# Another table of priorities for the planned instruction order of an attention and two feed-forward layers

## The chip, the cores and the metric

The kernel runs on one core of a Trainium2 chip. The metric is the device time of one execution in microseconds (us). TensorE, VectorE, ScalarE, GpSimd and SyncE appear in the views as PE, DVE, ACT, POOL and SP; PEld is the loading of weights into PE, and SPq is SP's queue of transfers.

## The reference

Attention in float32 over 2 batches of 8 heads, 768 positions and 64 dimensions, where a query sees only the keys of its own hash bucket, then a gated layer of width 1536 behind a normalisation, then a layer of width 2048:

```python
q_bits = (np.einsum('bhsd,dk->bhsk', q, proj) > 0)          # 6 bits make the bucket
mask = q_bucket[:, :, :, None] == k_bucket[:, :, None, :]
scores = np.where(mask, scale * np.matmul(q, k.transpose(0, 1, 3, 2)), -1e9)
attn = softmax(scores);  x = np.matmul(attn, v)             # (1536, 512) tokens
xn = x / rms(x) * rms_g
x = (silu(xn @ w_gate) * (xn @ w_val)) @ w_out              # 512 -> 1536 -> 512
return (np.maximum(x @ w_in, 0) ** 2) @ w_out2              # 512 -> 2048 -> 512
```

## The kernel before, in words

**Attention** goes in 96 slots: 16 heads with 6 tiles of 128 queries each. A slot is a short chain over the engines. PE makes the scores of the tile (`S`, L627: four matmuls of 384 columns, two parts of the operands by two halves of the keys). DVE takes their maximum and copies them out of PSUM (L638, `Pa` or `Px`). ACT makes the bias (L647) and the exponentials (L656). Then the probabilities are split into two 16-bit parts and transposed, by one of two ways. In the "a" slots, 66 of them, ACT makes the high part (`hla`, L376), POOL the low part by a subtraction (L385, `hla<-Pa,hla`), and a DMA on SP's queue transposes both (`Ta`, L668). In the 30 "x" slots PE transposes (L675), ACT and DVE read the result out of PSUM. Last, PE multiplies with the values (`O`, L701, 18 matmuls).

**Each head** needs its own preparation ahead of its first slot: loads of keys (`rk`, L466, 384 KB) and queries (`rq`, L469, 192 KB), the split of keys and queries into a high part (L378, L376 or L380) and a low part (L385, `k<-rk,k` and `q<-rq,q`), a hash by PE (L508), its bits by DVE (L517, `q<-S,cst`), and a small DMA that brings the bits to the keys (L525). Values are loaded for two heads at a time (`vr`, L552, 384 KB), scaled (L603) and split (L380 or L376 and, for the low part, L385, `vl<-vr,ones`).

**The normalisation** of a half batch (L940 to L975) makes the sums of squares on ACT (L940), scales them on DVE (L945), raises them to -1/2 on POOL (L950) and corrects the result by one Newton step in four small DVE instructions (L957, L959, L961 and L965, which writes `rr`). Three tiles of `xall` are then multiplied by `rr`, on DVE (L973), ACT (L971) or POOL (L975); PE transposes them (L983), and ACT and DVE split them into `xTA` (L991, L389). Only behind the normalisation of the first half can the first layer's products start (L1122 into the hidden units, L1234 and L1245 out of them). Weights come as 64-bit numbers (`wraw`, L1053, 512 KB a block) and are made into two parts by ACT, DVE and POOL (L1066 to L1086, L376, L385).

**The order** of all this isn't written by hand. `plan_all` gives each operation a rank, the engines that may run it, and a cost. `Plan.shift` adds a number from the table `SHIFTS` to each rank, and `Plan.run` is a list scheduler: it emits, one after the other, the ready operation that can start first by the costs, and on a tie the one with the lowest rank. Which engine runs an operation, and each engine's order, come out of that. The order is fixed at build time; on the chip each engine takes its instructions in that order and waits on semaphores.

```python
moved = int.from_bytes(raw[2 * n:2 * n + 2], "little", signed=True)
o.rank = (round(o.rank * 32) + moved) / 32 + n * 1e-6
...
if best is None or (t, o.rank) < best[0]:
    best = (t, o.rank), n, eng, c
```

37 matmuls on a tile of zeros (`idle`, L455) stand between the first slots.

Of the kernel before, what the change touches and what calls it, by code (L numbers as in the profile page):

```python
# [109 lines left out]


SHIFTS = (
    'c-rk(XLMCX*WOdktw0h==t##<rAw6>qy-QHO7ERF2nYfax)dW-q?Z5+2!tXv2neCPAQ&M60VEL+L%26LLUQjtWoGtw)_'
    'VWF-@otQw-(P{XU#fu*37JR_I{pu_GD}<8i<iZqt!xZj7OnShLdK5GDC}uQ&>IpFcisu58VkZG)mfYdqRg*sZc<V4HKA'
    'abRj>HGIEo+EYn3CuCe;bcg14shH*fgG<J*G#w1ZzZzz|Oxnh7doeY;xMVz%qJQ4q5SIkqgmhhW(MKttQOf)pnYAKb~1'
    'wB@jxFURJW$S>s6Mhu$V}|p*AbK?`8Dq_J#&(gee}%j7o`@3PT2*Bqu~oQKHV%^~tVnS{4zuEEH!;iViGARNl480w2nU'
    ')^<Uw37_rM|R5A%C7nr<hvNto<ZSM;Wi=gN;mog?+hP|M+WwDm3_rD=IcrRxB&r_8`OSc12p8<q_QF$;#MZ{<e$9jym*'
    'U@;tH_oV}tVh}r$I@VKcPq!GqVsG9OCP0FbVH9EqjKJAuU6`Ynqtn%oxB$1Q!RkxAu6LJ9RC6^SZ>e8lzFLNr;I<Kje5'
    'iw;+I!8!nwC=y!G73I?N&dS=`dfOg#f(|6QQD7Nfwd2a)j1N)m9$qHjdC5SOqO~>MP(&C`ryKO{L;NbyKVmUQ&Q9;2q3'
    '_Y;{&HwNL$v^i{gK!i*uY&ed|SbE4`l;>BEeqzXwM-h?*T7qeAsM-;gwd+RAG0%9Q3h;`KCC$+np1J2VtdRF$8sn&<Gq'  # L120
    'Rba5qMex^J{?8{B*hg&PS9PP8k=b<e8lsNOqQi3sg2mj>MnD{5;8_sHeZv`a<F-oe}Pl*s!>K7)_S@{b}?@_pQ#jel(n'
    '_?S#f5R+$o#VmN?32z|P?lW1Uu=wbmz?k+2Z|3NMq>%yc>d%8NKdl1TPM-vZ@fXt*;>6MggvXj(aVM6co{;!`kjt@z9w'
    'F0adcGg(MA*P1Sp^<Tt9^`1EjTEdS~=?jD*zcXH#k04PmqRN<0&9!2u`94-=?~oz-cj^XKGppP6*i>$_N}$WUq$-mBdN'
    'le)7qf^sXB-#H#b0nM`~~9@%u;3psAav8hjF_Zg$v*hbyU4j2lPhzr=p2-CryCv_#rkomZ@}kLF^J!g%^ryi|k5kt36b'
    'abc2kxEU`<UCN4UjkcKP?ljJ_JR6hq*jD{)$DjUn>Ju(uT<0E~MK2{%(BUvVCB2Sv@^lD}rT+>gZ4zKi6m_-J_5j8^Jt'
    '=H6AkqBxSmB=vC*_eXYttMJCtr}xST~YvVjBP|3%U~?NubKQJ-y~jA8B75WAWzYc;0Z&(67L~f9SZc;-Z0!SdK+_$RH('
    '=r8fCoY$a8(Jaa$jv=fW%(vUFVOec_!>B1i`Po6Uwcq-5|o^d-$yf;S!F*iinx{(y}jMRk*}!kU=nu^Fmer&ake_??V2'
    'i`o06^D%sM;ZaqbGzsnz705*pMLOVq-k5Dtr;Tw$!!d;qaE07z%`~packr%}CU-z8b}sA>|CXJtXXXS0p(pg`d&xJXm;'
    'OGUk{zu|g$s=RbhW-2yU<8zXspJjqLR_vDrQ8Hu~=5^#i8nZJKLr)nRG(U9EL#7$Yz*m9G3UhT=Nd3s=x6ATx?vlPN+J'
    '@a`rWTC7Wr#VX@F3tgjKL*5Ly^4KDJ=&Qj1y41|B!V7roQ*gU?@+_2G1BwO)omBoBgiYaO_p2RtrD^poj`9i!jpNkZ%h'  # L130
    '@*rPdw@s%K{G{x<rej^FC7T$WtbV(WKo3O79-GN+x2FuDYh}&v1B|Zj$5}?S#p%_wmQny;+cw3<;6Rqv5K)-+EbMi4Xi'
    '@;C)IGL^_6I4^P>&+#8k6}jOQ0=zW7;Olcz{u%OxArkE{&Ql(qAm7yCqgbzFk*T1V6e)_rl1wj-0|G<Hp16t~16kst@-'
    'D)A{%a8UGR<v|lA1;gPaO$9|w)=EXm9lW*2DMzYtY&}NWafNh)ljJj8<(`3Ku`y`KL-$l=H?Vv)nbzU2$zyc!7`#eb%R'
    '9Du_J&yPCB#B)_eC5^YT;{jBwU3qqTdIL@>g_6@E>xMeiE$2@8Ck>lyNv&wX`x}KLGoQ_7jt>{%WF1Rwq>tzL`EYdUz6'
    'KX)z04Vm9qXQ(Z~!Xw^?Og~}Mu6!l^?j8qNOJeWoo28Zx#&RA7NWs^?u2~EQY8Yv&Chs3GwSyN;e_OV@6ztR%KfKzlfo'
    '2Dw_Ok9Ce=mgS|g=t@vE90RB3=A)kW7uw5pH-6sNN?Dnl4J|zVOiv!ED2?0KP-@y>0K<uaWam6ta9)JSPstcD^*<`l^4'
    'hz(UIIyQ$!3Ipl->4Y$}JtbJVRH<e@w%_sPwoGXs2RmWE4msN5qbVs++JznJ-WPz<v(6oo&L-{4&=!2N2e+(1TPEy%_='
    'Eyg{Fe`qkZT1}Vxz>SljK2frb3aD@GnR_alb*E)9&oNKlkzcZB+6(5V*ObAFl7FBT|K9nK{z5gC<Ge&Nn2(P!j?$TQKH'
    '0=O8^!gRW*O&ZdKI>?O{}TW1(Ntn{f@X2-m8C3zaZyGA|GZB(KAGpF`r$gSIGufjJet9Z%oxH&{%q!EaK&iG~<?5TMLp'
    'VtT-*^4r^QW^G2Lrfp=hANRW?l%rUkZXZZ=1O+TkWGQsr)spGk>Ro3FQNUa^qq({keepPGhK&_S*rWM#h@`U{DsNksX+'  # L140
    'QED9POLPYMGre3I{Rx!ctxIz*I^|&<4BTCwIPlvtSAeSZz3DYsgAp5M4%Nd%lztj#0RoA4#f^?r<rU7^5*ejydr*#zgk'
    'MH*PiB8XYaCFWI)tW`9v(#qIkBwY83q;@|wJ?UDi@qbyk!wp*{0UJErnnk&K)r@Oku@iiJ9yLIqxqRb?319SHb8q%B;v'
    'n1|QpBe5l$&o8qbdC%xES~@?`S&o%rFG#&WN47FAj}37u`Z4?&covxCJB8~5S$R#_;=ChhD;(c|7Xqt&?for$Pt{r~ZO'
    '#=05`2sOqy2+?Q)x4PHvfG7^}M32M#0`UJqtPnCl?zKTJ1XT%GI+9y^-1aPVa8lP)}@;*7&98v3sJ+>8|J9;TrELQ6OD'
    'ig9ltu1w}nGJw-g9dHUg*H<Pq=TJwVP?lInmnBhufMG8*1UU-)|_dB-->xa7)Obq|4u&h;8FRC2DCfW;iIXotuQ!q>2k'
    'aOg7(V2D#ZpR4Chf%=<ZIk)|33BoYZqh60_ec$OMue<GkSxZMWEP2yWjh*_SLIfjiAAuNdO=QN7W!#C-r%b-l|3Qf&?('
    'y2auVw!yUB<0k)5|CHaBnLyY#u-L1(BNfFc$XFc<e?TT&hC<8}Pb5pUnoy^OC|H#tPDhaBmX4X`{MRjtT0FjOkE(8{_i'
    'Vj*p8XZ-?ABgIK9Ug3YLL{^F(BlWcFo}H>3&QhcB6$Y$cHjfkJ8kq$b)DV%VvM?X(i92FBPg0StxstGV#3;uex8JEtH}'
    '<fdSJ<)CDxz(}-$Ze>)j5ohq^5{r<B3Oga@NNtBFkoUST4~nh~?TTd;lvQlbk<k?HmPSF#imTc;dn3yo*&yAC8*R20LE'
    'T@s8t=>rQcQ)C3spwrcKt2FH#0{5GV!lW?FX7o1+xuBkX!>b(RB-VOMeyyAcH!`$s?Z)|dIg=<=jcR3U@hSU4*#qQT`l'  # L150
    'UH^942`{WoErNT);Olpy5tt!BHG*TYpmvVmvMRAiL9oU%%Vx0b88g9czv#`rLz?;#}Db3$R3!b^>Z^akBp}`v~hF+RJY'
    'yaLK;hYX>G}e<TxyYkaiQ&5XnZZHuO>NmB_&gCC<WY>rhl{{H=H$Oo%!R5LMj00MBDAo`g9#2BNh;aWCw_=c=UkJFX=)'
    ';TP2fo{E@=dl4^W`-lT<k@}mQR<&VH;Ai+<_EMad2pEA9`3ca7Wfgl;tdTgGx6$@vgr3jK3|zp?=A)vqVo9;q5o_3ZF%'
    'qiqNQcw0&KK=SAbF1YWNYAaQX_vObXBz+=Ny}SeqUd*&p&}24YXDd^3%!GKolJvI7j|^bv`dhudyf`@#YonotNXhOCP8'
    ')d8M%2n}K+kto8Nved%B7@BON*{|${IJ&D5MuX22c{8Rn9zl9nP+g0{IAGv0bG&(hW4Q8_%>@04iNw`-=<VnA<!{>{~8'
    'MLSEvs&RIYpQRkty6{I3pUF4t1uS6I_-PvGklXp-G92$GNd)@O}FF5;CkC5tXG{e(UA#-v<)4Nnq!2q91F-vXh%DRV(9'
    '05Cw)z-ku@}hym5?Ulzzugk*?$%-Y@J3(d1)N19mx2SqbE#yMW!sDcWab23g6blS$eFI*W6@h<9OcNEg>OR>k=_&oJ(g'
    '4!Bu!k|Q?1^C41eOUJMij;G+@|0d7KLOPDT%eT|wcr@pNtd3`~6?Q4?jAx)D|Bb)LyK9MXh(E@9aD`unOVEm@l5AV6M`'
    '<l>H&lYHWHVWU{t<O+En&2(N(Zs_j(8%V61O0i<&baj9L?2#BwfQjZ5{1Fy*!C7#$(ut?;>ez5UmDVY`-Rn5o%8D2JlU'
    'Ldu=AMAd^<5|E6=owcr+=Lb6Fe=%$iGv2X^qk{<SrRE58%>(HC@Qs?P;93FbC((oSMR!MeOH3XKkXvhve#7<BZMq|lP5'  # L160
    'EJn|Iu`t7nwo>Jh%NzAXaw|NYv30#7U#h}^9#5k(x5F#w~8|^T<|-+j6a7`FeP*bx7&TiD!B`PvU<>)R&mtn04x;kaTP'
    '@341A!Lsw;&%^kS&VeKsf7S!=D+>M34;^+q(_H>*M;E2u7!DEpKx!KY+4Rx3Pi9KnHD*H~!1FmBoYtq5e;9q4~zE?iUp'
# [1318 lines left out]
```

## Time and profile before

| | us |
|---|---|
| median of 3 runs | 787.13 (787.03 to 789.05) |
| the profiled execution | 786.7 |
| its span, first to last instruction | 784.9 |
| PE busy | 761.1 (97%) |
| PEld busy | 690.0 (88%) |
| DVE busy | 686.5 (87%) |
| ACT busy | 452.6 (58%) |
| POOL busy | 230.6 (29%) |

The time of an execution is its span and 1.8 us around it. Busy time of PE counts each matmul from its issue to its end, and neighbours overlap, so 97% isn't PE at its peak. The granted clock is the share of TensorE's full 2.4 GHz that the chip allowed in a stretch; 0.50 is its lower level, 1.2 GHz. "Idle before" in an instruction's row is the time in which its engine stood still ahead of it, with the one that ended it.

### The profile page before, as it was taken

The page shows a single profiled execution, that of the slowest core. Times are in us where ns is not written, and L with a number is a line of the kernel's source. Part 1 is how long each engine was busy: PE and PEld are TensorE (multiplying, and loading weights), DVE is VectorE, ACT ScalarE, POOL GpSimd, SP SyncE. Part 2 cuts the span into 40 slices and gives each one's busy share as a digit, 9 for nine tenths or more (in the row PEclk, how much of TensorE's full clock was granted, in tenths as well). Part 3 has the DMA queues.
Part 4 walks back from the last instruction along what each step waited for, and adds up shares of the span by engine and source line. Part 5 has one row for each costly group of instructions (what it writes and reads, how often), then busy time and mean ns, then how long its engine had stood idle before and what let it go on. Part 6 is the DMA issues. An engine that isn't in the chain of part 4 may idle for free.

```text
span 784.9 us, 14412 instructions
## 1 busy us (share of the span) xinstructions
PE 761.1 (97%) x5401; PEld 690.0 (88%) x5401; DVE 686.5 (87%) x1341; ACT 452.6 (58%) x897; POOL 230.6 (29%) x196
## 2 busy tenths in 40 slices
...
GB/s 251 130 172 169 207 153 141 143 190 195 230 205 163 198 164 197 97 129 164 108 146 96 134 139 134 130 82 130 58 54 53 54 108 53 54 55 53 28 1 161
DMA packets 127726, 100.65 MB, mean 128 GB/s; under 512 B 106548, under 2 KB 108596, under 8 KB 127656
## 3 DMA queue, kind: packets, MB, share of 16 engines
...
## 4 chain that ended last, share of the span: by engine, by line
PE 76%; DVE 11%; ACT 5%; DMA 4%; issue 2%; POOL 1%; SPq 0%; ACTq 0%; DVEq 0%; POOLq 0%
PE mo L1122 37%; PE mo L1245 17%; PE mo L1234 12%; PE S L627 4%; PE O L701 3%; DMA Ta<-hla 3%; DVE Pa L638 2%; DMA wraw<-in_w 1%; PE S L508 1%; DVE Px L638 1%; DVE Tx L385 1%; ACT Px L656 1%; ACT Pa L656 1%; ACT hla L376 1%; PE mo L455 1%
## 5 line engine op out<-in xcount | busy, mean ns | idle before, releaser
L1122 PE MATMUL mo<-xTA,wih 128*128 128x384 f32 (+1 forms) x512 | 138.4, 351 | 0.0
L1122 PE MATMUL mo<-xTD,wih 128*128 128x384 f32 (+1 forms) x512 | 136.8, 348 | 0.0
L385 POOL TENSOR_TENSOR hla<-Pa,hla 128x768 f16<-128x768 f32 x66 | 112.3, 1704 | 68.3 <-ACT hla L376 58.8
L1261 DVE TENSOR_TENSOR acc<-acc,mo 128x512 f32<-128x512 f32 (+1 forms) x164 | 100.9, 617 | 22.2 <-PE mo L1245 17.5
L1122 PEld LDWEIGHTS mo<-xTD,wih 128*128 128x128 f32 x512 | 93.3, 188 | 5.0
L1122 PEld LDWEIGHTS mo<-xTA,wih 128*128 128x128 f32 x512 | 92.8, 188 | 5.0
L1158 ACT ACTIVATE mt<-mo 128x512 f32<-128x512 f32 x48 | 28.7, 598 | 117.6 <-PE mo L1122 117.5
L627 PE MATMUL S<-k,q 76*128 76x384 f32 (+1 forms) x384 | 87.0, 354 | 6.3 <-DVE Px L638 2.8
L380 POOL TENSOR_SCALAR wih<-wv 128x512 fp32r<-128x512 f32 x16 | 9.9, 622 | 278.1 <-DVE wv L1086 265.3
L1122 PE MATMUL mo<-xTA,wil 128*128 128x384 f32 (+1 forms) x256 | 89.4, 349 | 0.0
L1122 PE MATMUL mo<-xTD,wil 128*128 128x384 f32 (+1 forms) x256 | 89.0, 348 | 0.0
L627 PEld LDWEIGHTS S<-k,q 76*128 76x128 f32 (+1 forms) x384 | 65.2, 190 | 10.9 <-DVE Pa L638 4.8
L1066 ACT ACTIVATE wv<-wraw 128x512 f32<-128x512 f32 x82 | 54.6, 671 | 21.0 <-DMA wraw<-in_w 19.2
L638 DVE TENSOR_SCALAR_CACHE_REDUCE Pa<-S 128x768 f32<-128x768 f32 x66 | 62.7, 950 | 3.5 <-PE S L627 2.6
L656 ACT ACTIVATE Pa<-Pa,b 128x768 f32<-128x768 f32 x66 | 62.3, 944 | 5.6 <-DVE ss L945 1.5
L1162 DVE TENSOR_TENSOR mu<-mt 128x512 f32<-128x512 f32 x48 | 33.3, 693 | 36.9 <-ACT mt L1158 36.9
L1234 PE MATMUL mo<-yl,woh 128*128 128x384 f32 x192 | 64.4, 335 | 1.2 <-DVE yl L385 1.2
L1234 PE MATMUL mo<-yh,woh 128*128 128x384 f32 x192 | 65.0, 339 | 0.3 <-DVE wol L385 0.3
L1234 PE MATMUL mo<-yh,wol 128*128 128x384 f32 x192 | 64.3, 335 | 0.0
L1082 DVE SCALAR_TENSOR_TENSOR wv<-wraw,wv 128x512 uint32<-128x512 uint32 x82 | 57.7, 708 | 1.0
L1086 DVE SCALAR_TENSOR_TENSOR wv<-wraw,wv 128x512 uint32<-128x512 uint32 x82 | 55.9, 686 | 0.4
L376 ACT CAST hla<-Pa 128x768 f16<-128x768 f32 x66 | 54.8, 834 | 2.2 <-DMA Ta<-hla 1.6
...
## 6 DMA issues: line engine op xcount, KB each, us to landing
wraw<-in_w SPq DMA_DIRECT2D x104, 512.0 KB
rk<-in_k SPq DMA_DIRECT2D x14, 384.0 KB
vr<-in_v SPq DMA_DIRECT2D x8, 384.0 KB
...
q<-q SPq DMA_DIRECT2D x15, 192.0 KB
rq<-in_q SPq DMA_DIRECT2D x14, 192.0 KB
Ta<-hla SPq DMA_TRANSPOSE x66
rk<-in_k ACTq DMA_DIRECT2D x2, 384.0 KB
```

The lines of the kernel that those rows point to most:

```text
L376: nc.scalar.copy(out_, in_)
L385: engine[eng].tensor_tensor(out=out_, in0=in0, in1=in1, op=ALU.subtract)
L627: nc.tensor.matmul(sp[:, hf, 0:TB], d[a][0:kr, t * 128:(t + 1) * 128], d[b2][0:kr, hf * TB:(hf + 1) * TB], start=(n == 0), stop=(n == 1),)
L638: nc.vector.tensor_scalar(out=e["P"].rearrange("p (a b) -> p a b", a=2), in0=e["sp"][:, :, 0:TB], scalar1=-1e9 / SCALE, scalar2=None, op0= ...
L656: nc.scalar.activation(e["P"], e["P"], AF.Exp, bias=e["b"], scale=SCALE)
L1066: nc.scalar.activation(t, f32(wst[m]["hi"]), AF.Abs)
L1082: nc.vector.scalar_tensor_tensor(out=t, in0=hi, scalar=0xC0000000, in1=t, op0=ALU.bitwise_and, op1=ALU.bitwise_or)
L1086: nc.vector.scalar_tensor_tensor(out=t, in0=lo, scalar=29, in1=t, op0=ALU.logical_shift_right, op1=ALU.bitwise_or)
L1122: nc.tensor.matmul(ps, a[:, c * 128:(c + 1) * 128], b2[:, c, :], start=(c == 0 and n == 0), stop=(c == 3 and n == 2),)
L1234: nc.tensor.matmul(po, a[:, dc * 128:(dc + 1) * 128], b2, start=(j == 0 and n == 0), stop=(j == len(fs) - 1 and n == 2),)
L1245: nc.tensor.matmul(po, a[:, tt * 128:(tt + 1) * 128], b2, start=(j == 0 and n == 0), stop=(j == len(fs) - 1 and n == 2),)
L1261: nc.vector.tensor_tensor(out=ac, in0=ac, in1=st["p"], op=ALU.add)
```

## The change

The table `SHIFTS` is another; nothing else is changed. Its rows are packed numbers and say nothing to a reader:

```diff
 SHIFTS = (
-    'c-rk(XLMCX*WOdktw0h==t##<rAw6>qy-QHO7ERF2nYfax)dW-q?Z5+2!tXv2neCPAQ&M60VEL+L%26LLUQjtWoGtw)_'
...
+    'c-rk(XLMFYx88eBdEb|WmIwrpA`um731A>dM>>cCQuKoa5RsyRPw666Kro;nQl+RADFGo!wNW(`gFr;86d{0+kn+CgoS'
...
 )
```

All operations are the same, and there are as many on PE (7160) as before. Nearly each engine's order is another. A few operations change engine: DVE has 1246 instructions (1247 before), ACT 897 (892), POOL 201 (201). The changed file is one line shorter above the code, so its line numbers are one lower: L384 there is L385 before.

**First place: DVE and POOL at the normalisation of the first half.** DVE before, from the scaled sums of squares (L945) to the multiplication of a tile (L973):

```order
L945 TENSOR_SCALAR ss<-ss 128x3
L638 TENSOR_SCALAR Pa,m<-S 128x768
L649 TENSOR_SCALAR b<-m 128x1
L957 TENSOR_TENSOR rt<-rr 128x3
L959 TENSOR_TENSOR rt<-rt,ss 128x3
L961 TENSOR_SCALAR rt<-rt 128x3
L517 TENSOR_SCALAR q_2353<-S,cst 44x768
L649 TENSOR_SCALAR b<-m 128x1
L945 TENSOR_SCALAR ss<-ss 128x3
L965 TENSOR_TENSOR rr<-rr,rt 128x3
L638 TENSOR_SCALAR Pa,m<-S 128x768
L973 TENSOR_SCALAR xall<-xall,rr 128x512
```

DVE now, from and to the same operations:

```order
L944 TENSOR_SCALAR ss<-ss 128x3
L564 TENSOR_REDUCE mx<-vr 128x1
L637 TENSOR_SCALAR Pa,m<-S 128x768
L956 TENSOR_TENSOR rt<-rr 128x3
L578 TENSOR_SCALAR mo<-mo 128x2
L958 TENSOR_TENSOR rt<-rt,ss 128x3
L583 TENSOR_SCALAR ma<-mo 128x2
L960 TENSOR_SCALAR rt<-rt 128x3
L588 RECIPROCAL sc<-ma 128x2
L964 TENSOR_TENSOR rr<-rr,rt 128x3
L648 TENSOR_SCALAR b<-m 128x1
L972 TENSOR_SCALAR xall<-xall,rr 128x512
```

The bits of a head's hash (L517, for which DVE waits on PE) stood between the third and the last Newton instruction; now it stands nine rows behind the multiplication. On POOL one low part of the probabilities (`hla`) stands between the two powers (L950) and so beside the multiplication, where there were two behind the second power.

**Second place: the low parts of the fifth head's keys and queries.** DVE before (`k_760` and `q_712` are that head's operands):

```order
L638 TENSOR_SCALAR Pa,m<-S 128x768
L385 TENSOR_TENSOR k_760<-rk,k_729 128x768
L385 TENSOR_TENSOR q_712<-rq,q_712 64x768
L385 TENSOR_TENSOR Tx<-mo,Tx 128x384
L638 TENSOR_SCALAR Px,m<-S 128x768
```

DVE now:

```order
L637 TENSOR_SCALAR Pa,m<-S 128x768
L384 TENSOR_TENSOR vl<-vr,ones 128x384
L384 TENSOR_TENSOR Tx<-mo,Tx 128x384
L637 TENSOR_SCALAR Px,m<-S 128x768
```

POOL now, where that head's parts went (`k_735` and `q_724` there):

```order
L384 TENSOR_TENSOR vl<-vr,ones 128x384
L384 TENSOR_TENSOR k_735<-rk,k_709 128x768
L384 TENSOR_TENSOR hla<-Pa,hla 128x768
L384 TENSOR_TENSOR q_724<-rq,q_724 64x768
L384 TENSOR_TENSOR hla<-Pa,hla 128x768
```

Two whole-tile subtractions left DVE for POOL, and a half-sized one of the values came to DVE instead.

**Third place: SP's queue ahead of the transposes of slots 48 and 49,** the first two "a" slots behind the middle of the program. Before:

```order
L525 DMA k_2198<-q_2062 12x768
L466 DMA rk<-in_k 128x768
L469 DMA rq<-in_q 64x768 x2
L552 DMA vr<-in_v 128x2x384
L668 DMA_TRANSPOSE Ta<-hla 128x12x128 x2
```

Now:

```order
L524 DMA k_2133<-q_2046 12x768
L465 DMA rk<-in_k 128x768 x2
L551 DMA vr<-in_v 128x2x384
L468 DMA rq<-in_q 64x768
L1052 DMA wraw<-in_w 128x512
L667 DMA_TRANSPOSE Ta<-hla 128x12x128 x2
```

One more load of keys and one block of weights stand ahead of the two transposes, and one load of queries less.

## Rows read from the trace of the kernel before

**Rows 1.** Busy us (and instructions) of each engine by stretch, granted clock, DMA share, GB/s
```profile
core 0: us, PE busy (x) PEld busy (x) DVE busy (x) ACT busy (x) POOL busy (x), PEclk, DMA share, GB/s
20.00:130.00 110.00, 101.11 (x1310) 90.42 (x1307) 103.36 (x225) 101.15 (x232) 82.28 (x65) 1.00 0.80 168
130.00:149.20 19.20, 14.44 (x107) 12.58 (x108) 14.96 (x34) 14.70 (x30) 13.07 (x13) 0.73 0.63 117
149.20:325.00 175.80, 172.24 (x1629) 166.33 (x1628) 167.92 (x321) 137.45 (x275) 101.83 (x72) 1.00 0.89 189
325.00:785.00 460.00, 456.09 (x2285) 410.69 (x2284) 383.66 (x721) 188.00 (x344) 21.75 (x30) 1.00 0.26 91
```
**Rows 2.** Waits of PE: total us, times, longest
```profile
PE O L701 <- DMA Ta<-hla: 4.8, 6, 1.1
PE S L627 <- DVE Px L638: 2.8, 2, 2.3
PE mo L983 <- DVE xall L973: 2.0, 1, 2.0
PE S L627 <- DMA k<-q: 1.2, 1, 1.2
```
**Rows 3.** Timeline at the first normalisation: start, us, instruction, [idle before <- what ended it]
```profile
133.56 0.55 DVE L961 TENSOR_SCALAR rt<-rt 128x3 f32<-128x3 f32 x1
135.92 1.08 DVE L517 TENSOR_SCALAR q<-S,cst 44x768 fp32r<-44x768 f32 x1 [1.81 <-PE S L508]
137.17 0.15 DVE L965 TENSOR_TENSOR rr<-rr,rt 128x3 f32<-128x3 f32 x1
138.98 3.23 POOL L385 TENSOR_TENSOR hla<-Pa,hla 128x768 f16<-128x768 f32 x2
139.03 3.46 DVE L973 TENSOR_SCALAR xall<-xall,rr 128x512 f32<-128x512 f32 x1
142.56 2.61 PE L983 MATMUL mo<-ident,xall 128*128 128x128 f32 x11 [2.01 <-DVE xall L973]
```
**Rows 4.** Two stretches of that place, same columns as Rows 1
```profile
132.90:136.30 3.40, 3.35 (x19) 3.05 (x20) 1.51 (x5) 2.90 (x6) 2.81 (x4) 0.51 0.43 80
139.80:146.60 6.80, 4.79 (x34) 4.22 (x34) 6.10 (x11) 3.78 (x8) 4.33 (x4) 0.50 1.11 185
```
**Rows 5.** Timeline at the fifth head's preparation, DVE, POOL and PE
```profile
40.44 1.54 DVE L385 TENSOR_TENSOR k<-rk,k 128x768 fp32r<-128x768 f32 x1
41.23 2.27 POOL L385 TENSOR_TENSOR hla<-Pa,hla 128x768 f16<-128x768 f32 x1
42.02 2.30 DVE L385 TENSOR_TENSOR q<-rq,q 64x768 fp32r<-64x768 f32 x1
45.83 0.44 PE L627 MATMUL S<-k,q 128*128 128x384 f32 x1 [2.34 <-DVE Px L638]
```
**Rows 6.** DVE groups by form, 0 to 325 us: count, busy, mean ns, idle before
```profile
L385 DVE TENSOR_TENSOR yl<-mu,yh 128x384 fp32r<-128x384 f32 x16 | 12.2, 775 | 0.0
```
**Rows 7.** The same form, 340 to 770 us
```profile
L385 DVE TENSOR_TENSOR yl<-mu,yh 128x384 fp32r<-128x384 f32 x29 | 15.6, 550 | 0.4 <-POOL yh L380 0.4
```
**Rows 8.** POOL groups by form, 0 to 325 us
```profile
L385 POOL TENSOR_TENSOR hla<-Pa,hla 128x768 f16<-128x768 f32 x66 | 112.3, 1704 | 68.3 <-ACT hla L376 58.8 <-ACT b L647 4.6 <-DVE xTA L389 1.9
L385 POOL TENSOR_TENSOR q<-rq,q 64x768 fp32r<-64x768 f32 x12 | 22.1, 1838 | 3.2 <-ACT q L376 1.8 <-PE O L701 0.6
L385 POOL TENSOR_TENSOR vl<-vr,ones 128x384 f16<-128x384 f32 x16 | 14.5, 912 | 2.7 <-ACT ones L376 2.5
```
**Rows 9.** SP's queue, the transposes of slots 48 and 49
```profile
127.13 5.44 SPq L668 DMA_TRANSPOSE Ta<-hla  x2
```
**Rows 10.** DMA issues: line, count, size of one
```profile
wraw<-in_w SPq DMA_DIRECT2D x104, 512.0 KB
rk<-in_k SPq DMA_DIRECT2D x14, 384.0 KB
rq<-in_q SPq DMA_DIRECT2D x14, 192.0 KB
```

More of the change, by code (lines that the diff above doesn't have):

```diff
@@ L112 @@
 SHIFTS = (
-    'c-rk(XLMCX*WOdktw0h==t##<rAw6>qy-QHO7ERF2nYfax)dW-q?Z5+2!tXv2neCPAQ&M60VEL+L%26LLUQjtWoGtw)_'
[L114 to L162, printed above, removed]
@@ L163 @@
-    '{mx;P0EjnFzz49x`cM35cbqxcgfxQn_P<jGz%~HLF9cX*k6Z2MGCalo1fZ+^{hYo2zj2EE@43acLT|LkAMA%h30r0UZ='
-    'moNZ}Apy@fL6K7XSb7Km7T4dj'
+    'c-rk(XLMFYx88eBdEb|WmIwrpA`um731A>dM>>cCQuKoa5RsyRPw666Kro;nQl+RADFGo!wNW(`gFr;86d{0+kn+CgoS'
+    'E7Cp1Z#L=dSPmxa<D8e|Tn{bJm%ev(8@g?AgyVspfdh679?%v_aEx1$HKjp1~AM5G$~jS)K@{;R$@xSP5OI1|2|?7W<>'
+    '0;nVn|$fWf&hHA>4@*ZTmZDqRqGxftxULn*_+pvjD!#Q3%BMy&Kf)URaXpYw7=r}EN$LJlfR1T1b#1whl+vv97-*k0dO'
+    '}FCOI+=F3sro&=g$nhTd{K4LeQCFssfO#BZk|&}x4?!6a6m6s4f#{uk>1fidXrSKbd<yST!@WjMfqK%0cB8S-JJJgeZ8'
@@ new lines @@
+    '1(aVyBc4)hDBF=9s?jqUI?+Nd_spAe&SRCVrzuaeEPtZzjHh}JWuP)(o=XHlkF&bhiR&Zc~8G^F{n6ZnSl8$1JN@kL#q'
+    'T59G3+Kjug1<b=;6c4Qef8kE=3$+z?@Oqvqt`=^=w!D?M_>s592$iR7-PSs8%`wv;B0qL&f`SS9Hd>eq)ePW7Zw}N!Ee'
+    '^T!aWOv+rHyjNRX_UQ#mAH=7jR9uX$|(q(E|CDH-PFzX2J?Q$i+NJ&k`+ghxfJUCQ2AC9^<=|f}ijKC`*T=A?~S)dJyH'
+    '|eqr-ncutQ~cOVzq`@D>$lQM_DqjV1ARcJ$F@K0_HzhMt9(k*l}1mQ9*lNyt$n|Mr|w|B!#IuD(&MR0;TfG=|ec|(`u>'
+    'ogWWg(xvWv<)VOj=)%b0+zT)7on=r(OB)(=Z^FYb$}wL7QMq;osQ%h7w}{6GtS}V`ejaVkNEsIbW3ufI-_s6rQiXbr7w'
@@ new lines @@
+    'BCo6p0=H{K#PIe@F(G|`Cn&=~G4D{-7Ch1>WfouT*L7lq(tN;Q|kPU<99d+C0D{=g%=N!-F1NB4}7%%@mmJv6{`{GuL9'
+    'JLn*F_IjI_jQezpPV)(VNhiYwSWW%;h<5^e;dNuE&g3R=miBQHY(@#?V1?YmN1?3_K|egNOT!$Pix=d0>Z~f5ON4+U+z'
+    ';aUC*2MrR0UQ+1=<L|!jm`#20>lbmWEJOXRqik8u_v9#9ZD4&vQxDUk!%&Dg=jMx1L2I^B7m=De6VlT}=k|v*sVrgXgG'
+    '~awVkFC$I)O<6X`$BroL{ecA7ER2DS1OG0DL)Q44XXr&MO+0cwn;uD4;B6^`@wLo8`Hvo)*qI6(^Xf5hMZJYs@#8h}%J'
+    'TB%zeR0cf3`2M-9o31HM|B|2t_tb+fX2}(GhV+3N5lyI7_PH_6usaiU7)wsApRVN2k*c*yn(}2z+9vr!#8k%u7WLt8?C'
@@ new lines @@
+    ')ORUL*CvLe2X@4`3sbu&NQ8C__uCc-P`SL&z0?7-<rl)ao&tQ%BYhjglbU2n&WTA4O(;jkLXmE~wZb6dkcy97n-dJr!;'
+    '@}#p2Mj7vlN`&G$_%kw`DmZzzQY#~AW)bwDpKX^@!sVT8ogfZEC%cK=z4&#GvzOZcupX)|P9OUrOfT+lxAkk<8M~#GXu'
+    'Cx#FkdXe11jE<<`Z@^aEjiuu3&2TvA}7}f?T7LJ-#ShbPGotH@LHC5X>&B6HeqWy|FZr62fIM4Zq;xK%;PG(Y|8Fdg2X'
+    'E6Q!Y#SD!Z9(~A~5C3$jDcgUmLMq{J2>V!iAX1KTGx`Q!Y#9}@T(w{oAFqSKLzraw)lpDE$&Y{*i;O%jB;Thh5opdMq9'
+    'P*r<&K(};ru#cI)g8kRRTBKp<=kFob$66eLCnxg;8oq*od#zEUEDbNwZ~o>XL#C~DDp%)jOEp`zf(&Ml(wy8sx07BViH'
@@ new lines @@
+    'sdJS$O_R;C&WVeH~&(NCN~Q)KVL_o1%PPPUgX<K4de6Na5>w4Pt^fD`0RZ@F{R`2qTQSDofmOV(D$=%lySDKF-^t!SW_'
+    '>u&M)?;Sd%SIKX}>k6MQ7*o*DXMQFhaF4tD-4_aH6z+7hyf{@(NF9-dxJic#&f?d6QAWv(!uEw$QDc#S*{+L^tLIf?Gg'
+    '&+>5+F{LRnc%CKUG7yjb4lC#IV!PK+WIE-p(ect9TU@AEJlUyl{U(VZktwEY9;zx=YR7r_^r+-Jl}0f$>z=8OejyX)h6'
+    'OVGofZ8>trZE$@5w@E+ELU9`Zj2HUU}kK_yZ2^M>G_?AlITsjC%v8;HRvoKdo;Ol%CD&tGuGQ5d9@hv>&P4+I!hF%m;!'
+    'iD%8Ho{%%L-)G6sT+v)(XWV={3MTb$E%T)j3c7^itYxg4sLgMGsj^>X;fH4u8lgS-T{yAJNtQp$WbfQUwV_g#2wr`Sxv'
```

27 lines of the change are left out of this document (added).

## Prediction

> **What bounds the kernel now.** I read the busy times by stretch first [rows 1]. From 325 us to the end PE is busy for 456.1 of 460 us at the full clock. What is left there, 3.9 us, is almost all the tail behind the last matmul (accumulation and the last stores), and the table changes neither. In those 460 us the order of the other engines is free as long as they keep up: DVE has 383.7 us of work for them. So the table can win or lose before 325 us alone. There PE stands idle for 8.9 us of the 110 from 20 to 130 (8.1%), for 4.8 us of the 19.2 from 130 to 149.2, and for 3.6 us of the 175.8 behind that. The reader is to see two things. The stretch from 149.2 us on, where products of the first layer fill PE between the slots, loses little (2%). And the dear place is 130 to 149.2 us: there the mean granted clock is 0.73 as well.
>
> Then the waits of PE [rows 2], to see who is late. They are many and short. PV waits for transposed probabilities (4.8 us in 6), scores wait for the DVE maximum that frees their PSUM (2.8 us), the transposes of the normalised tokens wait for DVE (2.0 us), and one score waits for the DMA of hash bits (1.2 us). No engine is the bound of the first 130 us alone: DVE is busy for 94% of 20 to 130 us, ACT for 92%, POOL for 75%.
>
> Then the timelines of the two longest waits. At 42 us DVE has both low parts of a head between two maxima [rows 5]. The keys take 1.54 us, the queries 2.30 us, while POOL runs an `hla` beside them that takes 2.27 us instead of its mean of 1.70 [rows 8]. The maximum that PE waits for comes behind, and PE stands for 2.34 us. At 139 us a multiplication on DVE (L973) starts 50 ns after the first of two `hla` on POOL and ends at 142.49, with the end of both [rows 3]; PE waits 2.01 us for it. So DVE and POOL hold each other up at SBUF. A larger sample says the same: `yl` takes 775 ns while POOL is busy [rows 6] and 550 ns when it hardly is [rows 7].
>
> The change, step by step, against the profiled execution of 786.7 us; that is 0.4 us under the median of 787.1, and I carry the difference over.
>
> **First place, the normalisation.** What it costs now: 4.8 us idle [rows 1], and two stretches at the lower clock level of 1.2 GHz, 0.51 and 0.50 of full, with 3.35 and 4.79 us of busy PE in them [rows 4]. At the full clock that work takes half as long, so they cost (3.35 + 4.79) / 2 = 4.1 us. Together 8.9 us in 19.2. A slice of this length at the rate of 20 to 130 us would lose 19.2 × 8.1% = 1.6 us.
>
> What the change does: the third Newton instruction ends at 133.56 + 0.55 = 134.11 us, and the fourth, which writes `rr`, starts at 137.17, 3.06 us later, since the hash bits stand between them and DVE waits 1.81 us for PE there [rows 3]. In the new order only one reciprocal of a few numbers is between the third and the fourth, and no wait for PE's hash. So `rr` comes 3.06 us earlier in its chain. That covers the 2.01 us for which PE waited behind L973, even if L973 meets POOL again: one `hla` is beside it now, 1.70 us, not two of 3.23 in all. So the wait goes: -2.0 us. The second low-clock stretch, from 139.8 us, has that wait in it; I take the stretch as gone with the wait, 4.79 / 2 = -2.4 us, and leave the first one, about which the order shows nothing. The freed time isn't free of waits: the usual 1.6 us of idle come back, since PE then waits for the next maximum on DVE. Sum -2.0 - 2.4 + 1.6 = -2.8 us. Bounds: nothing gained (0) and all 8.9 us.
>
> **Second place, the head's low parts.** DVE loses 1.54 + 2.30 = 3.84 us of work between two maxima and gets `vl` for it. DVE's own row nearest to that one is a two-input subtraction of the same 384 columns, 550 ns undisturbed [rows 7] and 775 in company [rows 6]; held behind a whole `hla` it would be 0.55 + 1.70 = 2.25 us. So DVE is freed of 1.6 to 3.3 us just ahead of the maximum, and the 2.34 us wait falls by 1.6 to 2.3. I take the near end, -1.6, because the new order still has POOL's `hla` beside `vl`.
>
> What it costs: POOL gets two parts of 1.84 us (the queries' row; the keys have as many columns) for one `vl` of 0.91 [rows 8], 2.8 us more between two `hla`. POOL has room, 110 - 82.3 = 27.7 us there [rows 1], but the transposes behind these `hla` go out later. If one PV more waits for it, that is about the longest of its kind, 1.1 us [rows 2]. I take 0, since queries for a head are due several slots ahead, and keep 1.1 for the range. Apart from this place the new DVE order has three whole low parts (queries once before the normalisation, keys and queries once each behind it), the old one two (queries, once before and once behind). One for one they cost alike, 0; the third falls where products fill PE, 0 as well.
>
> **Third place, SP's queue.** One load of keys (384 KB) and one weight block (512) more and one load of queries (192) less stand ahead of two transposes [rows 10]: 704 KB more. At the 168 GB/s of 20 to 130 us [rows 1] that is 4.3 us of transfer. It costs nothing if the loads go out as soon as their buffers are free, ahead of the `hla` that the transposes wait for anyway: these were issued at 127.13 us [rows 9]. It costs up to 4.3 us if not. I take 0, as four loads stood there before as well and these transposes' PV is one wait of six at most.
>
> **All else** is redrawn too: the other waits before 149 us. The order names no winner there: 0, with the six PV waits, 4.8 us, as what could go or double in both directions.
>
> Sum: -2.8 - 1.6 = -4.4 us. 786.7 - 4.4 = 782.3, and against the median of 787.1 it is **782.7 us**, 0.56% less. A difference under 0.3%, 2.4 us, can't be told from none here.
>
> **The rivals.**
>
> *The port is the bound, and waits only change sides* (25%). What DVE doesn't wait for POOL, POOL waits for DVE: the `hla` at 41.23 us paid 0.57 us over its mean beside the keys. POOL and the DVE instructions that need the same way into SBUF are as many as before, so their sum stays. For it: both engines' rows at 42 us are stretched. Against it: POOL fills 75% of 20 to 130 us [rows 1], so a quarter is left for DVE's share. Price: the two gains shrink to under 2 us in sum, so 785 to 788, 787 at the likeliest. The Trainium skill has a rule for this (SBUF — State Buffer, section "Who interferes with whom"): VectorE in certain modes or with two SBUF inputs and GpSimd hold a shared port pair by an exclusive lock for the whole instruction, and the other blocks fully. By that rule the sum of port time is fixed by the instructions, not by their order. The trace agrees with the lock, by the 3.46 us of L973; that its total bounds the kernel is shown by no row.
>
> *Late transposes* (15%), the slower side. The new queue in front of slots 48 and 49 delays them by the 4.3 us, just where PE has no products yet to put in between. PE then waits, the clock falls to 1.2 GHz as it does now, and the first place gains nothing. 787.1 - 1.6 + 4.3 = 789.8 us. It decides if the weight block's buffer comes free later than the `hla` of slot 48. For it: the two transposes held SP for 5.44 us already [rows 9], so the DMA engines were crowded. Against it: none of PV's six waits is over 1.1 us [rows 2].
>
> *Everything at the first place goes* (12%). Both low-clock stretches and all waits there, 8.9 us, and the whole 2.3 us of the second place: 787.1 - 11.2 = 775.9 us. For it: the only low-clock stretches of the program stand amid its densest waits, so fewer waits may spare both. Against it: with DVE busy for 94% of the time before, slots without waits are unlikely.
>
> **How the numbers follow.** The forecast has 48%, with 780 to 784.7 as its own range (the second place at either end, the usual idle or none coming back). Faster by over 0.3%: 48 + 12 = 60%. Within it: 25%. Slower: 15%. The range goes from 777 (the first place at its bound of 8.9, the second at -1.6 and one PV wait more is 777.7) to 790 (the late transposes); outside are most of the third rival and the worse half of the second, under 2 in 10.
>
> **What would show it.** Right: PE idle of 130 to 149 us falls from 4.8 to about 2, one stretch at the lower clock instead of two, first product (L1122) some 3 us earlier than 149.2; no PE wait over 2 us at a maximum behind a head's low part; PE still full from about 325 us on. Wrong: the two stretches stay or move to another place; PV waits sum to more than 4.8 us; DVE's L973 takes over 3 us again. The forecast as a whole is wrong if the idle time before the first product, 13.7 us from 20 us on, is the same, wherever it lies.

## The result, and the profile after

The changed kernel takes **779.11 us** (median of 5 runs, 777.28 to 782.5) where the kernel before took 787.13 (5 runs): a ratio of 0.9894, 95% interval 0.9858 to 0.993. In a later comparison it was 777.11 against 787.31, 0.9888 (0.9872 to 0.9904). So 8 to 9 us are gained, where 4.4 were forecast; both medians lie in the range of the prediction, the later one at its edge (777 to 790). The profiled execution took 781.1 us, its span is 779.3 (before 784.9). Line numbers are one lower than before: L972 is the old L973.

Busy time by stretch (columns as in [rows 1]):

```profile
20.00:130.00 110.00, 102.30 (x1315) 91.39 (x1314) 101.42 (x236) 105.19 (x243) 85.04 (x66) 1.00 0.80 170
130.00:149.20 19.20, 18.82 (x164) 17.98 (x165) 14.89 (x32) 16.80 (x32) 15.47 (x13) 0.92 0.85 147
149.20:325.00 175.80, 171.69 (x1584) 164.59 (x1584) 162.81 (x326) 135.82 (x275) 100.06 (x75) 0.99 0.93 187
325.00:785.00 460.00, 450.53 (x2250) 405.17 (x2248) 377.77 (x707) 182.51 (x331) 17.69 (x25) 1.00 0.25 90
```

The reader is to see the idle time of PE, first number less second: 7.7 us from 20 to 130 (before 8.9), 0.4 from 130 to 149.2 (4.8), 4.1 from 149.2 to 325 (3.6). The last row ends at 779.3 us, so that 3.8 us are idle there, the tail; before, up to 784.9 us, there were 3.8 as well.

The waits of PE (total, times, longest), the four largest of the whole span:

```profile
PE O L700 <- DMA Ta<-hla: 4.4, 6, 1.0
PE S L626 <- DVE Pa L637: 2.1, 5, 0.6
PE S L626 <- DVE q L516: 1.6, 2, 1.3
PE mo L454 <- DVE half L1387: 1.0, 1, 1.0
```

The two long ones of [rows 2] are gone, 2.3 us at a maximum and 2.0 us at L973. PV's waits for transposes are about as they were. Nothing is longer than 1.3 us in this execution; in the later profiled one, a PV wait near 77 us took 1.9.

The two stretches at the lower clock level in this execution (columns as above):

```profile
129.50:132.90 3.40, 3.23 (x13) 2.94 (x14) 2.77 (x8) 3.40 (x9) 2.53 (x4) 0.50 0.59 114
180.70:184.10 3.40, 3.40 (x11) 3.40 (x12) 2.13 (x8) 2.73 (x10) 3.13 (x4) 0.50 1.10 225
```

Before there were 10.2 us at this level in the first normalisation [rows 4], now there are 3.4; the second stretch above is not in the later profiled execution of the same kernel. Every run lists its mean granted clock: 0.9922 over the 23 runs of before in the later comparison, 0.9964 over the changed kernel's ten. At two levels that is 2 × 0.0078 × 787 = 12.3 us at 1.2 GHz against 2 × 0.0036 × 778 = 5.6, and half of the difference, by this estimate up to 3.3 us, is time saved where PE was busy.

The later profiled execution of the changed kernel is 775.0 us long, 9.9 less than that of before. PE is busy for 757.3 us of it, so 17.7 us are idle where it was 23.8: 6.1 us less. At the lower level it has one stretch:

```profile
127.60:130.90 3.30, 3.27 (x26) 2.97 (x27) 3.30 (x11) 3.30 (x8) 2.78 (x3) 0.50 0.12 27
```

PE is busy for 3.27 us in it; before, the two stretches had 8.14 [rows 4]. Half of the difference, an estimate, is 2.4 us. So idle time and clock together make up 8.5 of the 9.9 us.

The first normalisation, timelines of DVE and POOL (start, us, instruction, what ended the idle time before):

```profile
128.18 0.16 DVE L964 TENSOR_TENSOR rr<-rr,rt 128x3 f32<-128x3 f32 x1
128.22 1.65 POOL L384 TENSOR_TENSOR hla<-Pa,hla 128x768 f16<-128x768 f32 x1 [0.92 <-ACT hla L375]
128.38 1.78 DVE L972 TENSOR_SCALAR xall<-xall,rr 128x512 f32<-128x512 f32 x1
129.87 1.31 POOL L602 TENSOR_SCALAR vr<-vr,sc 128x384 f32<-128x384 f32 x2
133.92 1.09 DVE L516 TENSOR_SCALAR q<-S,cst 44x768 fp32r<-44x768 f32 x1 [0.21 <-PE S L507]
```

The instruction that writes `rr` starts at 128.18 us, not at 137.17 [rows 3], and the hash bits come 5.7 us behind it. L972 follows `rr` at once, still meets an `hla`, and takes 1.78 us where L973 took 3.46. It ends 0.29 us behind that one `hla`.

The fifth head's preparation, the same view:

```profile
39.96 1.83 POOL L384 TENSOR_TENSOR k<-rk,k 128x768 fp32r<-128x768 f32 x1
41.95 0.55 DVE L384 TENSOR_TENSOR vl<-vr,ones 128x384 f16<-128x384 f32 x1
43.90 0.95 DVE L637 TENSOR_SCALAR_CACHE_REDUCE Px<-S 128x768 f32<-128x768 f32 x1
44.11 1.83 POOL L384 TENSOR_TENSOR q<-rq,q 64x768 fp32r<-64x768 f32 x1
```

Both low parts are on POOL. `vl` on DVE starts between POOL's key part (to 41.79) and its next `hla` (from 42.27) and is not held up. The wait of 2.34 us [rows 5] is gone.

Last, a group of DVE and one of POOL, 0 to 325 us (count, busy, mean ns):

```profile
L384 DVE TENSOR_TENSOR yl<-mu,yh 128x384 fp32r<-128x384 f32 x17 | 9.8, 589 | 0.9 <-ACT yh L375 0.9
L384 POOL TENSOR_TENSOR hla<-Pa,hla 128x768 f16<-128x768 f32 x66 | 111.2, 1686 | 69.1 <-ACT hla L375 50.6 <-DVE acc L1260 5.8 <-DVE Pa L637 3.4
```

`yl` takes 589 ns where it took 775 [rows 6], and 66 `hla` take 1686 on the mean, not 1704 [rows 8]. All of DVE's work takes 672.7 us of the span instead of 686.5, with the same operations but for some that changed engines. The two engines hold each other up less.

### The profile page after: what moved, and what is told of

It reads as the page before. It is cut to its first block, busy times and chain, and to the rows that moved or that the text cites. A ratio compares the mean times of both kernels' runs of the same rounds, so it can differ in the third digit from the quotient of the medians.

```text
span 779.3 us, 14432 instructions
## 1 busy us (share of the span) xinstructions
PE 761.0 (98%) x5401; PEld 689.8 (89%) x5401; DVE 672.7 (86%) x1340; ACT 451.1 (58%) x898; POOL 230.7 (30%) x196
## 4 chain that ended last, share of the span: by engine, by line
PE 77%; DVE 7%; ACT 6%; DMA 4%; issue 3%; POOL 2%; SPq 0%; ACTq 0%; POOLq 0%; DVEq 0%
PE mo L1121 38%; PE mo L1244 17%; PE mo L1233 12%; PE S L626 4%; PE O L700 4%; DMA Ta<-hla 3%; DVE Pa L637 1%; ACT hla L375 1%; POOL hla L384 1%; PE mo L674 1%; DVE Px L637 1%; ACT Pa L655 1%; ACT xall L722 1%; DMA wraw<-in_w 1%; ACT Px L655 1%
## 5 line engine op out<-in xcount | busy, mean ns | idle before, releaser
L384 POOL TENSOR_TENSOR hla<-Pa,hla 128x768 f16<-128x768 f32 x66 | 111.2, 1686 | 69.1 <-ACT hla L375 50.6
```

The source lines that it names most:

```text
L384: engine[eng].tensor_tensor(out=out_, in0=in0, in1=in1, op=ALU.subtract)
```

## The experiments

Each kernel was timed in 5 rounds beside the kernel before. The numbers in the edits count the planned operations as the program makes them: 829 is the fourth Newton step (L965), 831 the scaling L973, 215 the last head's hash bits (L517); 113 and 114 are the fifth head's low parts of keys and queries, 94 and 107 the low parts of the third and fourth head's values, 409 and 433 low parts `Tx`, 441 and 898 `hla`, 152 a maximum `mx` (L565), 230 a cast of queries (L380), 460 a row maximum, 885 the scores of slot 50, 1337 the first product (L1122). `move` changes the place in the list of operations, `engine_of` the engine.

**One instruction alone, L965 ahead of the hash bits.**

```diff
-        for o in plan.run():
+        all_ops = list(plan.ops)
+        seq = plan.run()
...
+        move(829, before=215)
+
+        for o in seq:
             o.fn(o.eng)
```

> The kernel before with one instruction moved: the fourth Newton instruction (L965, writes rr) ahead of the hash bits of the last head (L517) on VectorE. Theory (the places named in the prediction make the gain): PE's wait for L973 falls from 2.0 us to under 0.5, the second stretch at the lower clock (139.8 to 146.6 us) is gone, the time falls by 2 to 3 us. Rival A (the two engines' shared way into SBUF is the bound, waits change sides): L973 still takes over 3 us, or another wait of that size appears before 150 us, time within 1 us of before. Rival B (the low-clock stretch is no consequence of this wait): the wait goes, the two low-clock stretches stay, the time falls by under 1 us.

Measured: 788.06 us, ratio 1.0004 (0.9984 to 1.0025). No gain is seen. Timelines of DVE and POOL:

```profile
134.47 0.35 DVE L965 TENSOR_TENSOR rr<-rr,rt 128x3 f32<-128x3 f32 x1
137.60 0.96 DVE L638 TENSOR_SCALAR_CACHE_REDUCE Pa<-S 128x768 f32<-128x768 f32 x1 [0.90 <-PE S L627]
138.42 3.24 POOL L385 TENSOR_TENSOR hla<-Pa,hla 128x768 f16<-128x768 f32 x2
138.48 3.46 DVE L973 TENSOR_SCALAR xall<-xall,rr 128x512 f32<-128x512 f32 x1
```

`rr` is ready at 134.8 us, and L973 starts at 138.48 all the same. It stands on DVE behind a maximum that waits for scores, and then it meets the same pair of `hla`, again for 3.46 us. PE waits 1.9 us for it, and the long low-clock stretch is there too:

```profile
139.14:145.96 6.82, 4.90 (x35) 4.33 (x34) 6.20 (x11) 3.79 (x8) 4.35 (x4) 0.50 1.09 186
```

Rival A's first sign is there: L973 takes over 3 us, and the time is, at the middle, within 1 us of before. When `rr` is ready doesn't set the time of L973. The low-clock stretch begins 0.94 us ahead of the wait (which is from 140.08 us on), so the wait didn't start it.

**L973 moved up as well.**

```diff
+        move(829, before=215)
+        move(831, before=215)
```

> The kernel before with two instructions of VectorE moved ahead of the hash bits L517: the fourth Newton instruction L965 and the scaling L973 that PE waits for. Theory (what costs is not rr's time alone but that L973 stands behind a maximum and then behind two hla in a row): L973 starts near 135 us and ends by 137, since one hla is beside it there and POOL's next instruction comes with a gap; PE's wait for it (1.9 us) goes, the low-clock stretch of 6.8 us is halved or gone, the time falls by 2 to 4 us. Rival (waits only change sides): the hash bits and the maximum behind them come 1 to 2 us later and PE waits there; time within 1 us of before.

Measured: 786.06 us, 0.9985 (0.9968 to 1.0001); at best 2.5 us, at the middle 1.2. L973 takes 0.49 us, PE waits no more for it, and 3.4 us are left of the low-clock stretch. But L965 now takes 1.57 us, since it starts beside an `hla`, so the hash bits come later, and the next scores wait for them. DVE's timeline:

```profile
135.83 1.57 DVE L965 TENSOR_TENSOR rr<-rr,rt 128x3 f32<-128x3 f32 x1
137.44 0.49 DVE L973 TENSOR_SCALAR xall<-xall,rr 128x512 f32<-128x512 f32 x1
137.96 1.08 DVE L517 TENSOR_SCALAR q<-S,cst 44x768 fp32r<-44x768 f32 x1
```

and PE's wait that is new:

```profile
PE S L627 <- DVE q L517: 1.9, 1, 1.9
```

The wait of 2.0 us went, one of 1.9 came: the rival's mechanism, with the theory's clock. Of the time neither forecast is settled: the interval reaches from nothing to 2.5 us.

**The pair of `hla` taken apart.** On POOL the cast L380 goes between them.

```diff
+        move(829, before=215)
+        move(898, before=230)
```

> As in the run with L965 alone moved, and on GpSimd the cast L380 of a head's queries moved from ahead of the two hla in a row to between them. Theory (a waiting VectorE instruction doesn't get in between two hla back to back, but does where another kind of instruction follows the hla): L973 ends 0.3 to 0.6 us behind the first hla, takes about 1.5 to 2.2 us instead of 3.46, and PE's wait for it falls by 1 to 1.9 us. Rival (the wait lasts as long as GpSimd has work without a gap): L973 still ends behind the second hla, 3.5 us or more.

Measured: 786.6 us, 0.9984 (0.9968 to 1.0001). DVE and POOL:

```profile
139.17 1.65 POOL L385 TENSOR_TENSOR hla<-Pa,hla 128x768 f16<-128x768 f32 x1
140.03 1.06 DVE L973 TENSOR_SCALAR xall<-xall,rr 128x512 f32<-128x512 f32 x1
140.79 0.99 POOL L380 TENSOR_SCALAR q<-rq 64x768 fp32r<-64x768 f32 x1
141.02 2.40 DVE L957 TENSOR_TENSOR rt<-rr 128x3 f32<-128x3 f32 x1
141.75 1.63 POOL L385 TENSOR_TENSOR hla<-Pa,hla 128x768 f16<-128x768 f32 x1
```

L973 ends at 141.09, 0.27 us behind the first `hla`, close to the theory's 0.3 to 0.6, and PE's wait for it is gone from the trace. (It takes 1.06 us and not the forecast 1.5 to 2.2, since it starts when half of that `hla` is done.) The next row is a lesson in itself: L957 works on three columns, starts beside the cast and takes 2.40 us, to the end of the second `hla`. It did not get in where the cast ended, though a different kind of instruction followed; so the theory's general part, that two `hla` in a row are what shuts DVE out, does not cover it. The hold-up passed on to the next instruction of DVE, where PE waits less for it. The time moved by 1.3 us at the middle of an interval that just reaches none.

**The head's parts alone.**

```diff
+        engine_of(113, "P")
+        engine_of(114, "P")
+        engine_of(94, "D")
+        move(113, after=107)
+        move(114, after=441)
+        move(94, before=409)
```

> The kernel before with three instructions on another engine: both low parts of the fifth head from VectorE to GpSimd, and the low part of the third head's values from GpSimd to VectorE. Theory: PE's wait of 2.3 us at 45.8 us falls to under 0.7, the stretch from 20 to 130 us ends 1.6 to 2.3 us earlier. Rival (GpSimd's 2.8 us more of work between two hla make a wait elsewhere): the 2.3 us wait goes and PV waits before 70 us grow by as much; time within 1 us of before.

Measured: 788.0 us, 1.0012 (0.9994 to 1.0031). The wait at 45 us fell from 2.34 to 0.57, as the theory said, and came back 7 us later. Rows of POOL, DVE and PE:

```profile
41.39 1.85 POOL L385 TENSOR_TENSOR k<-rk,k 128x768 fp32r<-128x768 f32 x1
41.42 2.22 DVE L385 TENSOR_TENSOR vl<-vr,ones 128x384 f16<-128x384 f32 x1
51.31 0.55 DVE L565 TENSOR_REDUCE mx<-vr 128x1 f32<-128x384 f32 x1 [1.96 <-DMA vr<-in_v]
51.78 0.55 DVE L385 TENSOR_TENSOR Tx<-mo,Tx 128x384 f16<-128x384 f32 x1
52.39 0.24 PE L701 MATMUL O<-ones,Tx 128*128 128x65 f16 x2 [2.08 <-DVE Tx L385]
```

`vl` on DVE starts 30 ns behind the key part on POOL and pays 2.22 us for it. At 51 us DVE stands 1.96 us at a maximum whose values have not arrived, with the `Tx` behind it for which PE waits. The clock falls behind that wait, from 53.7 to 57.1 us.

**The same, with that maximum behind `Tx`.**

```diff
...
+        move(152, after=433)
```

> The head's run again (both low parts of the fifth head on GpSimd, the third head's value part on VectorE), with one row of VectorE exchanged: the maximum L565, which there waited 1.96 us for a load of values, goes behind the low part of the transposed probabilities (L385) that PE waited for. Theory (the gain at 45 us was real, and was given back by that queue): PE's wait of 2.1 us for Tx at 52 us falls to under 1, the low-clock stretch at 53.7 us goes, the time is 1 to 2.5 us under before. Rival (VectorE and GpSimd have no room, the gain goes elsewhere): within 1 us of before.

Measured: 788.01 us, 1.0007 (0.9987 to 1.0026). The wait for `Tx` fell under 1 us, as the theory said, and another took its place. The low-clock stretch stayed as well (55.3 to 58.7 us). One row of POOL, one of SP, one of PE:

```profile
48.47 1.66 POOL L385 TENSOR_TENSOR hla<-Pa,hla 128x768 f16<-128x768 f32 x1
49.66 3.93 SPq L668 DMA_TRANSPOSE Ta<-hla  x2
54.13 0.20 PE L701 MATMUL O<-ones,Ta 128*128 128x65 f16 x1 [2.28 <-DMA Ta<-hla]
```

The `hla` that started at 44.60 us before starts at 48.47 here, behind the two parts that POOL got. 2.3 of the 3.9 us are that this whole execution runs later (the scores of the two slots ahead of it start at 43.07 us, before at 40.73); about 1.5 us are the two parts. So its transposes go out later, and the PV that waited 0.99 us for them before waits 2.28. That is the rival of the first run of this edit: POOL has room on the mean, but not between these two `hla`.

**Both places together.** The edits of the second and of the fifth run.

```diff
+        move(829, before=215)
+        move(831, before=215)
+        engine_of(113, "P")
+        engine_of(114, "P")
...
+        move(152, after=433)
```

> Both edits together: L965 and L973 ahead of the hash bits, and the head's low parts with the exchanged row. Theory (the two places add up, as the prediction had them: 4.4 us): 3 to 6 us under before. Rival: within 1.5 us of before, so that the changed kernel's gain needs the whole sequence.

Measured: 787.86 us, 1.0 (0.9978 to 1.0022). The rival holds: the two places that the prediction named, as these edits make them, bring no gain that shows in the sequence of before (1.7 us at most). The trace has PV's wait with 2.4 us and the scores' wait for the hash bits with 1.9, as the two runs alone had them.

**The changed sequence in pieces.** Four kernels hold both tables, plan with each, and take one sequence up to a given operation and the other behind it:

```diff
+        one = plan.run(SHIFTS)
...
+        two = plan.run(SHIFTS_REST)
+        cut = one.index(all_ops[1337])
+        front = one[:cut]
+        done = set(front)
+        rest = [o for o in two if o not in done]
...
+        seq = front + rest
```

Changed up to the first product (1337):

> The changed kernel's sequence up to the first input projection of the first layer, the sequence of before behind it. Theory (the whole gain is made before 149 us, where PE has no products to fill in): the time is within 1.5 us of the changed kernel's, 7 to 9 us under before. Rival (a good part of the gain is made where products and slots are mixed, 149 to 325 us): 3 to 6 us under before.

Changed behind it only:

> The sequence of before up to the first input projection of the first layer, the changed kernel's behind it. Theory (gain made before 149 us): within 1 us of before. Rival (mixed stretch counts): 2 to 5 us under before.

Changed up to the scores of slot 50 (885), about 121 us:

> The changed kernel's sequence up to the scores of slot 50 (about 121 us), the sequence of before from there on, the normalisation with it. Theory (the normalisation makes the larger part of the gain): 1 to 3 us under before, with PE's wait for L973 and the low-clock stretch near 140 us as before. Rival (the gain is made ahead of it): 4 to 6 us under before.

Changed from there on:

> The reverse: the sequence of before up to the scores of slot 50, the changed kernel's from there on. Theory (the normalisation makes the larger part of the gain): 3 to 6 us under before, no wait for L973 over 0.5 us. Rival (the sequence behind 121 us pays only with the state that the changed first part leaves): within 1.5 us of before.

And the changed kernel whole, in the comparison with the last two:

> The changed kernel once more, beside the other runs: 7 to 9 us under before.

| to 121 us | 121 us to the first product | behind it | us | ratio (95%) | of 787 us |
|---|---|---|---|---|---|
| changed | before | before | 783.56 | 0.9965 (0.9948 to 0.9982) | -2.8 |
| changed | changed | before | 782.16 | 0.9934 (0.9907 to 0.996) | -5.2 |
| changed | changed | changed | 777.11 | 0.9888 (0.9872 to 0.9904) | -8.8 |
| before | changed | changed | 783.34 | 0.9959 (0.9936 to 0.9983) | -3.2 |
| before | before | changed | 789.91 | 1.0027 (1.0005 to 1.0048) | +2.1 |

Read down, each piece adds to the one ahead of it, though the step of the middle one, 2.4 us, is not clear of none. The last piece alone makes the kernel slower; behind the other two it gains 3.6 us (uncertain by 2.4). The middle piece, with the normalisation, is worth 5.2 - 2.8 = 2.4 us in front of the old rest and 2.1 + 3.2 = 5.3 in front of the new one (each uncertain by 2.5, the two intervals' half-widths added in squares). The first piece is worth 2.8 alone and 8.8 - 3.2 = 5.6 with the others. Of the first pair, the changed front alone gives 5.2 us, the rival's size (3 to 6), and the whole kernel gains 3.6 more; the changed rest alone is slower, which neither side forecast. Of the last pair both forecasts of the theory came in (2.8 us in 1 to 3, 3.2 in 3 to 6), but not what they were to show, that the normalisation makes the larger part: both halves gain some 3 us alone, and together nearly 3 more than their sum (8.8 against 6.0), which is about what the intervals allow as chance.

The mean granted clock of the runs says where that excess may lie. For the changed kernel it is 0.9974 here (0.9954 in the first comparison), for before 0.9922 beside it; by estimate that is up to 0.0052 × 782 = 4.1 us of its 8.8. Of the four pieces none has a clock more than 0.0009 over that of before beside it, which is 0.7 us. So by these means the pieces gain by less waiting, and only the whole gains by the clock as well. Why the whole order is spared the lower level no run shows.

The row of L973 on DVE (L1032 in these kernels, the file being longer), with the old normalisation behind the changed front:

```profile
135.68 3.46 DVE L1032 TENSOR_SCALAR xall<-xall,rr 128x512 f32<-128x512 f32 x1
```

and with the changed normalisation behind the old front:

```profile
133.07 0.79 DVE L1032 TENSOR_SCALAR xall<-xall,rr 128x512 f32<-128x512 f32 x1
```

The hold-up goes with the piece that has it. (Behind the old front PE waits 1.4 us for ACT's scaling instead.)

**The head's edit undone in the changed kernel.**

```diff
+        engine_of(113, "D")
+        engine_of(114, "D")
+        engine_of(94, "P")
+        move(113, after=460)
+        move(114, after=113)
```

> The changed kernel with the head's edit undone: both low parts of the fifth head on VectorE again, behind the same maximum as before, the value part of the third head on GpSimd. Theory (in the changed sequence this place is worth what the prediction gave it): PE waits some 2 us near 45 us again, 1.6 to 2.3 us over the changed kernel. Rival (as in the sequence of before, it is worth nothing): within 0.8 us of the changed kernel.

Measured: 780.38 us, 0.9923 (0.991 to 0.9935), 0.35% over the changed kernel's 0.9888 beside it, which is 2.8 us, uncertain by 1.6. DVE's rows and PE's wait:

```profile
41.43 0.96 DVE L384 TENSOR_TENSOR k<-rk,k 128x768 fp32r<-128x768 f32 x1
42.42 2.30 DVE L384 TENSOR_TENSOR q<-rq,q 64x768 fp32r<-64x768 f32 x1
44.74 0.56 DVE L384 TENSOR_TENSOR Tx<-mo,Tx 128x384 f16<-128x384 f32 x1
```

```profile
PE mo L454 <- DVE Tx L384: 1.9, 1, 1.9
```

The wait is back with 1.9 us, and behind it a stretch at the lower clock that the changed kernel lacks:

```profile
47.16:50.56 3.40, 3.40 (x30) 3.09 (x28) 2.42 (x6) 2.55 (x7) 1.16 (x2) 0.50 1.09 146
```

PE was busy all through it, so it costs 1.7 us in this execution. A second such stretch (81.3 to 84.7 us) stands behind a PV wait of 1.7 us; in the later profiled execution of the changed kernel a PV wait of 1.9 us near there had none. So a wait of this length is not always followed by the lower level. The theory holds: the same three instructions that bring no gain in the old sequence are worth some 2.8 us in the new one, wait and clock together. What differs there can be read, though no run isolates it: on POOL a cast of queries (0.83 us) no longer stands ahead of the key part, so that `vl` finds the key part done, and the `hla` behind both parts starts at 46.02 us, not at 47.15 or 48.47. Counted from the scores of the two slots ahead of it, that is 3.7 us in the changed kernel and 5.4 in both runs of this edit in the old sequence; before it was 3.9.

## Why the prediction was right, and where its size was off

**Where time can be won: right.** Behind 325 us nothing moved but the end (idle 3.8 us in both). The idle time from 20 us to the first product was 13.7 us; in the changed kernel it is 8.0 (columns of the second row as in [rows 1]):

```profile
135.87 0.51 PE L1121 MATMUL mo<-xTA,wih 128*128 128x384 f32 x2
20.00:135.87 115.87, 107.83 (x1356) 96.75 (x1356) 106.30 (x248) 111.06 (x255) 89.69 (x71) 0.99 0.78 164
```

The first product is 13.3 us earlier (135.87 us, not 149.17) and not 3, partly because the new order puts it ahead of the scores of three slots, which I had not seen.

**First place: the size nearly right, the reason wrong, so that the size is in part luck.** The term was -2.8 us; the pieces say -2.4 to -5.3 for all that lies between 121 us and the first product, and no run isolates the normalisation in the new order. "One stretch at the lower clock instead of two" came true there, and idle fell to 0.4 us, not 2. What failed is the step "So `rr` comes 3.06 us earlier in its chain. That covers the 2.01 us". With `rr` 2.7 us early and nothing else, L973 took 3.46 us again, PE waited 1.9 us, and the time stayed. L973 was bound by its own place, behind a maximum and beside two `hla` in a row. I had allowed for one `hla` beside it and took its length as the price, and that part is what the changed kernel shows (1.78 us). The clock's term failed as well: "I take the stretch as gone with the wait". The stretch began at 139.8 us and the wait only at 140.55 (2.01 us up to 142.56 [rows 3]); in the two runs that took this wait away at this place alone, 3.4 of the 6.8 us stayed, and in the run with both places all 6.8 (139.8 to 146.6 us).

**Second place: right in the new sequence, -1.6 forecast, -2.8 measured.** The difference is within the uncertainty (1.6 us); the trace puts 1.7 us of clock beside the wait, which I had counted at the first place only, since in the profiled execution of before the clock did not fall there. (With the same wait it did, from 46.98 us on in the first experiment and from 46.45 on in the second.) In the old sequence the step "I take 0" for POOL's 2.8 us, with 1.1 kept for the range, failed: the `hla` came about 1.5 us later, and a PV that had waited 0.99 us waited 2.28. I had taken the longest wait seen as the price, though a delay comes on top of a wait that is there.

**Third place: right.** PV's waits are 4.4 us in six, the longest 1.0; late transposes did not come. The two transposes go out at 123.64 us, where it was 127.13 [rows 9], though more loads stand ahead of them:

```profile
123.64 7.68 SPq L667 DMA_TRANSPOSE Ta<-hla  x2
```

What I had not seen in the new order: two loads of keys and two of queries left SP's queue for ACT's (4 of 16 each go out there, where it was 2). No run tries that alone.

**"All else 0": wrong.** 8.8 less 2.8 for the head and 2.4 to 5.3 for the normalisation leaves 0.7 to 3.6 us. The clock of the whole, up to 4.1 us by the estimate above, is of that size. The shorter `yl` behind the first product (186 ns in each of 17 instructions, 3.2 us of DVE's time) does not explain it: in the run with the changed order behind the first product only, `yl` takes 561 ns, and that kernel is 2.1 us slower than before. I had argued that the order names no winner, which was true of what I could read in it, but no reason for 0.

**The rival "the port is the bound, and waits only change sides"** describes every single edit in the old sequence: five kernels, none over 1.3 us at the middle. (Its sign, the 3.46 us of L973, was more than a hold-up by one `hla` gives; see the last section.) As a statement on the whole it fell. The sum of time in which DVE and POOL hold each other up isn't fixed by the instructions: nearly the same work took DVE 13.8 us less. As I read it, the price depends on which instruction of the one starts just behind one of the other, and that is what an order sets. DVE's time alone doesn't set the kernel's, though: the slower run just named has 4.4 us less of it than before (682.1).

**"Everything at the first place goes"** had 775.9 us, nearer to the later median (777.1) than the forecast. But the time came from three pieces, not from one.

No version here beats the changed kernel.
